# Other batches' mixing matrices on GpSimd, a later value chunk, and a fifth early product group in an attention and feed-forward kernel

## The chip, the cores and the metric

The kernel runs on one core of a Trainium2 chip. A core has five engines with an instruction queue each: TensorE (PE in the profile, with its weight loads as PEld), VectorE (DVE), ScalarE (ACT), GpSimd (POOL) and SyncE (SP). Each engine takes its instructions in order; semaphores order them between engines. Matrix products land in PSUM, which has eight banks of 2 KB for each of 128 partitions; GpSimd doesn't reach PSUM. The metric is the time of the whole program on the device in microseconds (us), lower is better. A profiled execution has a span, from the first to the last instruction that the profile shows, and a time of its own that is a little longer.

## The reference

Four batches, eight heads, 768 positions, head width 64. A sequence is cut into 8 blocks of 96. Per batch and head an 8x8 matrix is made from `sort_net` by five rounds of exponential and row and column normalisation; it mixes the key blocks and the value blocks. Attention then runs inside each block, and its output, heads side by side, goes through a gated feed-forward layer.

```
for _ in range(5):
    P = P - max(P, -1);  P = exp(P)
    P = P / (sum(P, -1) + 1e-09);  P = P / (sum(P, -2) + 1e-09)
k_sorted = einsum('bhij,bhjcd->bhicd', P, k_b)     # 8 blocks of 96 positions
v_sorted = einsum('bhij,bhjcd->bhicd', P, v_b)
attn = softmax(q_b @ k_sorted^T / 8);  x = attn @ v_sorted
x: 3072 tokens x 512
out = (silu(x @ w_gate) * (x @ w_val)) @ w_out      # 512 -> 1536 -> 512
```

## The kernel before, in words

Everything is in bfloat16 on the way into TensorE. The tokens are taken in eight groups of 384 (half a batch); a group `ffn(n)` has twelve gate products and twelve value products (four matmuls of 128x384 each, one for each 128 of the 512 channels `kc`), and the output products of the group before it. `gate_out` (L416) is a tanh on ScalarE (L420) and a product on VectorE (L422); `value_out` (L434) is one more product on VectorE (L435).

Attention is cut into units of two heads and four blocks. For a unit, `qk` makes the scores on TensorE (L334) and their exponentials on ScalarE (L345, L347); `av` (L353) averages the values on TensorE (L361), and VectorE divides by the sums with a reciprocal (L365) and a product (L367). For batch 0 the result is transposed on TensorE (L378) into x, drained to SBUF by a copy.

Before that, keys and values of batch 0 are mixed by TensorE: `w_ps` (L497) holds the spread 8x8 matrices of all batches, and `mix_rows` (L501) multiplies it by a 0/1 mask into the block matrices `rmix`, for batch 0 first and for batches 1 to 3 after the first scores (L524). `v_chunk` (L295) mixes 8 or 16 of the 64 value channels at a time, `k0_chunk` (L280) some of the 48 key positions of each half, `q0_chunk` (L271) only transposes q. Each chunk ends in a cast out of PSUM, on VectorE ("v") or ScalarE ("s") as its argument says. q of batch 0 is loaded in two halves; the second (`load_q0(1)`, L178) is used by `q0_chunk(1, ...)` (L634).

PSUM is shared out by tags: "a" and "b" are tiles of two banks, "gen" is three single banks in turn, "x" is one bank. A tile is given out again when the last reader of the one before it is done.

The order of the work in the opening (up to L573) is written out by hand for TensorE, GpSimd, VectorE and ScalarE. While x arrives slice by slice (`x_first`, L536), `early` (L546) runs matmuls of the first four products of group 0 (gates 0 and 1, values 0 and 1) for those slices that are there; the fourth has half of a two-bank tile "a". From L574 on the order is by hand for TensorE, GpSimd, ScalarE and SyncE, and a scheduler places VectorE's work. There `merge` (L604) lays side work into a product group by due times: a product counts 0.65, and a piece of side work is taken once the count has reached its due time. `units(0, range(4, 8), ...)` (L577, L637) is the second half of batch 0 in group 0: scores of two units, an average after 1.9 and 3.6, and the transpose 3.1 after each average.

The loads of weights, k, q and v are issued by GpSimd's queue in the order of the code; eight transfers can be under way, and the next waits for the oldest to land.

Of the kernel before, what the change touches and what calls it, by code (L numbers as in the profile page):

```python
# [10 lines left out]
BF16 = mybir.dt.bfloat16  # L11
# [6 lines left out]
def kernel(  # L18
# [11 lines left out]
    nc = tc.nc  # L30
# [80 lines left out]
    def load_k(b, lo, hi):  # L111
        load_groups(kq_tile(b), highr, k_nat[b], lo, hi)
# [5 lines left out]
    def load_q(b, lo, hi):  # L118
        load_groups(kq_tile(b), lowr, q_nat[b], lo, hi)
# [60 lines left out]
    load_gv(1024, DF)  # L180
    load_v(1, 0, 2)
    load_v(1, 2, 4)
    for lo, hi in ((0, 2), (2, 4)):
        load_k(1, lo, hi)
        load_q(1, lo, hi)
    for n in range(3):
        nc.gpsimd.dma_start(out=wo_sb[n], in_=wo_dram[:, n * 4:(n + 1) * 4, :])

    rmix = {b: const.tile([128, 2, H, NB], BF16, name=f"rmix{b}") for b in (0, 1, "p")}
    for t in rmix.values():  # L190
# [18 lines left out]
    rowreds = [const.tile([BH, NB, 1], FP32, name=f"rowred{it}") for it in range(N_ITER)]  # L209
    colred = const.tile([BH, 1, NB], FP32)  # L210
    p_bf = const.tile([BH, NB, 4, NB], BF16)
    def pair_tile(name, tag):
        return psum.tile([128, 1024], FP32, name=name, tag=tag)

    def bank_tile(name, tag="gen"):
        return psum.tile([128, 512], FP32, name=name, tag=tag, bufs=3 if tag == "gen" else 1)
# [54 lines left out]
    def q0_chunk(t, at, n, eng, tag):  # L271
        dst = kqt_tile(0)[:, GI * C:2 * GI * C].rearrange("p (g t r c) -> p t g r c", g=H2, t=2, c=QC)[:, t]
        tp = chunk_tile("tq0", n // 8, tag).rearrange("p (l g r) -> p l g r", l=n, g=H2)
        for lc in range(n):
            for two in range(2):
                nc.tensor.matmul(tp[two * D:(two + 1) * D, lc], lhsT=q0[t][:, at + lc, :],  # L276
                                 rhs=sel[:, two], start=True, stop=True)
        drain(eng, dst[:, :, :, at:at + n], tp.rearrange("p l g r -> p g r l"))

    def k0_chunk(at, n, eng, tag, parts=None):  # L280
        dst = kqt_tile(0)[:, 0:GI * C].rearrange("p (n a c) -> p a n c", a=2, c=HC)
        rm = rmix[0].rearrange("p a (g two) i -> p two a g i", two=2)
        tp = chunk_tile("tk0", n // 8, tag).rearrange("p (l a n) -> p l a n", l=n, a=2)
        for lc in range(n):
            for two in range(2):
                nc.tensor.matmul(tp[two * D:(two + 1) * D, lc].rearrange("p a (g i) -> p a g i", g=H2),
                                 lhsT=k0[:, at + lc, :], rhs=rm[:, two], start=True, stop=True)
        src = tp.rearrange("p l a n -> p a n l")
        if parts is None:
            drain(eng, dst[:, :, :, at:at + n], src)  # L290
            return
        drain(eng, dst[:, :, 0:parts, at:at + n], src[:, :, 0:parts])
        return lambda e: drain(e, dst[:, :, parts:, at:at + n], src[:, :, parts:])

    def v_chunk(b, at, n, eng, tag):  # L295
        rows = slice(0, 128) if b % 2 else lowr
        dst = vt_tile(b // 2)[:, b % 2]
        mix = rmix[b][rows, 0].rearrange("p a b -> p (a b)")
        tp = chunk_tile("tv", n // 8, tag).rearrange("p (l n) -> p l n", n=H * NB)
        for ld in range(n):  # L300
            col = (at + ld) * C
# [175 lines left out]
    def fill(tile, n):  # L477
        for _ in range(n):
            nc.tensor.matmul(tile, lhsT=warm_sb[:, 0:128], rhs=warm_sb, start=True, stop=True)  # L479
# [18 lines left out]
                             lhsT=p_bf[:, i].rearrange("p a b -> p (a b)"),  # L498
                             rhs=ident[0:BH, 0:BH], start=True, stop=True)

    def mix_rows(dst, rows, b):  # L501
        nc.vector.tensor_tensor(dst, mask[rows].unsqueeze(2).to_broadcast([R, H, NB]),
                                w_ps[rows, :, b].transpose([0, 2, 1]), op=ALU.mult)

    mix_rows(rmix[0][lowr, 0], lowr, 0)
    mix_rows(rmix[0][highr, 1], highr, 0)
    q0_chunk(0, 0, 16, "s", "b")
    v_chunk(0, 0, 8, "v", "gen")
    v_chunk(0, 8, 8, "s", "gen")
    v_chunk(0, 16, 16, "v", "a")  # L510
    v_chunk(0, 32, 8, "v", "gen")
    v_chunk(0, 40, 16, "s", "b")
    v_chunk(0, 56, 8, "s", "gen")
    q0_chunk(0, 16, 8, "v", "x")
    k0_chunk(0, 16, "s", "a")
    k0_chunk(16, 16, "v", "b")
    rest = [k0_chunk(at, 8, "s", "gen", 2 * NB) for at in (32, 40)]
    for drain_rest in rest:
        drain_rest("v")
    idle_ps = bank_tile("idle_ps", "x")  # L520
    fill(idle_ps, 3)
    qk(0, 0, "a")
    qk(0, 1, "b")
    for b in range(1, B):  # L524
        rows = halves[b % 2]
        mix_rows(rmix["p"][rows, b % 2] if b > 1 else rmix[1][rows, 0], rows, b)
    qk(0, 2, "gen")
    fill(idle_ps, 1)
    av(0, 0, "a")
    fill(idle_ps, 2)  # L530
    av(0, 1, "b")
    xts[(0, 0)] = xtp.tile([128, H2, TW], BF16, name="xt0_0", tag="xt")
    qk(0, 3, "mixed")
    av(0, 2, "a")

    def x_first(u, eng, tag):  # L536
        x_ps = xt_tile(tag, 1)[:, 0]
# [1 line left out]
        drain(eng, xts[(0, 0)][:, u, :], x_ps.rearrange("p a b -> p (a b)"))  # L539

    x_first(0, "s", "gen")
    x_first(1, "s", "gen")
    av(0, 3, "b")
    first = {}

    def early(n, kcs):  # L546
        sb, m, name = ((wg_sb, 0, "g_ps"), (wv_sb, 0, "v_ps"), (wg_sb, 1, "g_ps"), (wv_sb, 1, "v_ps"))[n]
        if n not in first:
            first[n] = (bank_tile(name) if n < 3 else pair_tile(name, "a"))[:, 0:TW]
        for kc in kcs:  # L550
            nc.tensor.matmul(first[n], lhsT=sb[:, kc, ts(m, 128)], rhs=xts[(0, 0)][:, kc, :],
                             start=(kc == 0), stop=(kc == NKC - 1))
# [2 lines left out]
    early(1, (0,))  # L555
    x_first(2, "s", "x")
    early(3, (0,))
    early(2, (0,))
    early(0, (1,))
    early(1, (1,))  # L560
    x_first(3, "v", "x")
    early(2, (1,))
    early(3, (1,))
    early(0, (2, 3))
    early(1, (2, 3))
    early(2, (2, 3))
    early(3, (2, 3))
    gate_out(0, 0, first[0])
    value_out(0, 0, first[1])
    gate_out(0, 1, first[2])  # L570
    value_out(0, 1, first[3])
    nc.vector.tensor_copy(rmix[1][lowr, 1].rearrange("p h i -> p (h i)"), ident[lowr, lowr])
    man.__exit__(None, None, None)  # L573
    man = tc.manual_schedule(engines={ET.PE, ET.Pool, ET.Activation, ET.SP})  # L574
# [42 lines left out]
    def ffn(n):  # L617
        todo = []
        for m in range(NFC):
            if n > 0 or m > 1:  # L620
                todo.append((0.65, lambda m=m: gate(n, m)))
                todo.append((0.65, lambda m=m: value(n, m)))
            ends = (7, 9, 11) if n == 1 else (3, 7, 11)
            if n > 0 and m in ends:
                for part in range(3):
                    todo.append((0.87, lambda t3=ends.index(m), part=part: outp(n - 1, t3, part)))
        return todo
# [62 lines left out]
```

## Time and profile before

| | us |
|---|---|
| median of three runs (lowest, highest) | 244.79 (244.59, 245.19) |
| the profiled execution | 244.99 |
| its span | 243.1 |
| TensorE busy | 235.4 |
| VectorE busy | 154.7 |
| ScalarE busy | 112.6 |
| GpSimd busy | 51.3 |

Times in the profile's rows are counted from the start of the span. A row of the timeline gives start, busy time, engine, line, operation, what it writes and reads, how many instructions it merges, and in brackets how long the engine sat idle before it and what ended that. A matmul's end is modelled and overlaps the next one's start, so the starts are what to read on TensorE.

### The profile page before, as it was taken

How to read it: one execution, taken by the hardware profiler on the slowest of the kernel's cores; microseconds unless marked ns; L12 is line 12 of the kernel's file. 1: busy time of each engine (PE TensorE's matmuls, PEld its weight loads, DVE VectorE, ACT ScalarE, POOL GpSimd, SP SyncE). 2: the span in 40 equal slices, each digit the busy share in tenths (PEclk: the TensorE clock that was granted, in tenths of full speed). 3: DMA queues.
4: the chain of work that ended last, by engine and by line, in shares of the span. 5: the costliest groups of instructions: out<-in, count | busy, mean ns of one | idle time of the engine just before them, and what ended most of it. 6: DMA issues, size and time to landing. Idle time of an engine off the chain costs nothing.

```text
span 243.1 us, 6156 instructions
## 1 busy us (share of the span) xinstructions
PE 235.4 (97%) x2613; PEld 138.5 (57%) x2613; DVE 154.7 (64%) x326; ACT 112.6 (46%) x191; POOL 51.3 (21%) x45
## 2 busy tenths in 40 slices
PE   7799999999999999999999999999999999999994
PEld 5375666676556566555555565565556555555543
DVE  6687789875665585866855855584576476445700
ACT  3976663486525544455453353254325434332312
POOL 5992229950006089000000000000000000000000
PEclk9999999999999999999999999999999999999999
DMA  5989999999926997543122212012111211110122
GB/s 93 214 131 209 206 213 212 205 210 193 156 78 107 219 177 109 109 95 81 49 72 61 47 45 80 0 59 63 32 43 49 73 36 43 43 43 3 43 86 86
DMA packets 39642, 24.77 MB, mean 102 GB/s; under 512 B 29376, under 2 KB 34368, under 8 KB 39616
## 3 DMA queue, kind: packets, MB, share of 16 engines
q0 software_dynamic: 19632, 14.16, 39.2%
q1 hardware_dynamic: 19840, 10.17, 15.8%
q8 instruction: 20, 0.33, 0.6%
q10 hardware_dynamic: 144, 0.07, 0.1%
q14 instruction: 6, 0.05, 0.1%
HBM read 28.32 MB, written 7.86 MB: 149 GB/s over the span
## 4 chain that ended last, share of the span: by engine, by line
PE 88%; DMA 6%; POOL 3%; DVE 1%; issue 0%; ACT 0%; POOLq 0%
PE v_ps L430 26%; PE g_ps L412 25%; PE o_ps L447 25%; DMA qk<-in_q_dram 4%; PE av_ps L361 3%; PE tkq L266 3%; PE qk L334 3%; POOL vch L148 3%; DMA v<-in_v_dram 2%; PE tv L312 1%; PE o_ps L463 1%; PE tv L302 1%; PE tq L276 0%; POOL wv_sb L134 0%; POOL wg_sb L134 0%
## 5 line engine op out<-in xcount | busy, mean ns | idle before, releaser
L422 DVE SCALAR_TENSOR_TENSOR gs_sb<-th_sb,g_ps 128x384 bf16<-128x384 bf16 x96 | 52.9, 552 | 50.8 <-ACT th_sb L420 47.8
L412 PE MATMUL g_ps<-xt,wg_sb 128*128 128x384 bf16 x376 | 76.6, 325 | 0.1
L430 PE MATMUL v_ps<-xt,wv_sb 128*128 128x384 bf16 x376 | 76.5, 326 | 0.0
L420 ACT ACTIVATE th_sb<-g_ps 128x384 bf16<-128x384 f32 x96 | 47.1, 491 | 57.3 <-PE g_ps L412 54.1
L447 PE MATMUL o_ps<-wo,h 128*128 128x512 bf16 x276 | 64.4, 379 | 0.0
L435 DVE SCALAR_TENSOR_TENSOR h<-v_ps,gs_sb 128x384 bf16<-128x384 f32 x96 | 53.4, 556 | 7.7 <-PE tkq L266 0.5
L412 PEld LDWEIGHTS <-wg_sb 128*128 128x128 bf16 x376 | 34.8, 97 | 23.4
L430 PEld LDWEIGHTS <-wv_sb 128*128 128x128 bf16 x376 | 35.0, 97 | 23.1 <-issue 0.2
L447 PEld LDWEIGHTS <-h 128*128 128x128 bf16 x276 | 26.0, 98 | 28.5
L452 ACT COPY o_sb<-o_ps 128x512 f32<-128x512 f32 x23 | 13.5, 586 | 49.3 <-PE o_ps L447 49.3
L148 POOL COPY vch<-v 64x1536 bf16<-64x1536 bf16 (+2 forms) x11 | 28.8, 2663 | 10.0 <-DMA v<-in_v_dram 10.0
L347 ACT ACTIVATE e_all<-qk 96x768 bf16<-96x768 f32 x30 | 23.2, 801 | 4.3 <-PE qk L334 4.3
L367 DVE TENSOR_TENSOR st<-av_ps,r_sb 96x512 bf16<-96x512 f32 x32 | 21.8, 680 | 0.3
L361 PEld LDWEIGHTS <-e_all 96*128 96x128 bf16 x256 | 11.9, 97 | 4.9 <-ACT e_all L347 0.6
L361 PE MATMUL av_ps<-vt,e_all 96*128 96x65 bf16 x256 | 13.0, 193 | 0.1
L246 ACT CAST vt<-tv 96x1024 bf16<-96x1024 f32 (+1 forms) x11 | 10.1, 931 | 4.7 <-PE tv L312 3.5
L365 DVE RECIPROCAL r_sb<-av_ps 96x8 f32<-96x8 f32 x32 | 6.4, 199 | 7.9 <-PE av_ps L361 7.9
L244 DVE CAST vt<-tv 96x1024 bf16<-96x1024 f32 (+1 forms) x7 | 7.4, 1065 | 2.2 <-PE tv L312 1.8
L479 PE MATMUL idle_ps<-warm_sb 128*128 128x512 bf16 x24 | 6.6, 382 | 0.0
L244 DVE COPY oq_v<-o_ps 128x128 f32<-128x128 f32 x1 | 0.3, 292 | 9.3 <-PE o_ps L463 9.3
L397 POOL DMA_DIRECT2D q_scr<-in_q_dram x2 | 5.6, 2813 | 0.3 <-issue 0.3
L146 ACT COPY vch<-v 64x768 bf16<-64x768 bf16 (+1 forms) x4 | 5.5, 1386 | 0.4 <-DMA v<-in_v_dram 0.4
(83 smaller groups left out, 130.5 us busy)
## 6 DMA issues: line engine op xcount, KB each, us to landing
out_dram<-o_sb SPq DMA_DIRECT2D x23, 256.0 KB, 2.0
v<-in_v_dram POOLq DMA_DIRECT2D x4, 384.0 KB, 12.7
wg_sb<-in_moe_w_gate_dram POOLq DMA_DIRECT2D x3, 512.0 KB, 11.2
wv_sb<-in_moe_w_val_dram POOLq DMA_DIRECT2D x3, 512.0 KB, 13.0
wo<-in_moe_w_out_dram POOLq DMA_DIRECT2D x3, 512.0 KB, 16.4
kqp<-in_k_dram POOLq DMA_DIRECT2D x2, 768.0 KB, 9.8
q_scr<-in_q_dram POOLq DMA_DIRECT2D x2, 768.0 KB, 17.4
v<-in_v_dram POOLq DMA_DIRECT2D x2, 768.0 KB, 9.8
```

Of the source, the lines that this page charges most:

```text
L148: eng.tensor_copy(dst, src.transpose([0, 2, 1]))
L246: nc.scalar.copy(dst, src)
L347: nc.scalar.activation(e_all[:, n:n + 2, 0:4 * C], wide[0:C, :, 0:4 * C], AF.Exp, scale=scale)
L361: nc.tensor.matmul(o[:, two, i4, 0:D + 1], lhsT=e[:, i4 * C:i4 * C + 128], rhs=vt[:, 2 * g + two, half * 4 + i4, 0:D + 1], start=True, sto ...
L367: nc.vector.tensor_tensor(st.rearrange("p i two d -> p two i d"), o[0:C, :, :, 0:D], r_sb.to_broadcast([C, 2, 4, D]), op=ALU.mult)
L412: nc.tensor.matmul(g_ps, lhsT=wg_sb[:, kc, ts(m, 128)], rhs=xt[:, kc, :], start=(kc == 0), stop=(kc == NKC - 1))
L420: nc.scalar.activation(th_sb, g_ps, AF.Tanh, scale=0.5)
L422: nc.vector.scalar_tensor_tensor(gs_sb, th_sb, 1.0, g_ps, op0=ALU.add, op1=ALU.mult)
L430: nc.tensor.matmul(v_ps, lhsT=wv_sb[:, kc, ts(m, 128)], rhs=xt[:, kc, :], start=(kc == 0), stop=(kc == NKC - 1))
L435: nc.vector.scalar_tensor_tensor(h_tiles[n][:, m, :], v_ps, 0.5, gs_tiles.pop(m), op0=ALU.mult, op1=ALU.mult)
L447: nc.tensor.matmul(o_ps, lhsT=h_w[:, m, ts(t3, 128)], rhs=wo_sb[part][:, m % 4, :], start=(m == 0), stop=(m == NFC - 1))
L452: nc.scalar.copy(o_sb, o_ps)
```

## The change

- `mix_rows` takes the engine and the source as arguments. Batch 0's matrices are still made by VectorE from `w_ps`. Right behind them VectorE copies the rest of `w_ps` to `w_sb` in SBUF, and GpSimd makes the matrices of batches 1 to 3 from that copy; they stand on its queue behind the loads of v of batch 1 and ahead of the loads of k and q of batch 1 and of the output weights.
- In the opening, the value chunk at channel 32 is drained by ScalarE, the small q chunk comes earlier, the two 8-wide key chunks come ahead of the two 16-wide ones, and the engines of these two are exchanged. The value chunk at channel 56 uses the bank "x" and stands behind the keys and the fills, and VectorE drains it.
- The first average stands ahead of the third unit's scores, and the first transposes stand ahead of the third and fourth averages.
- `early` runs five products: gate 2 joins, in the other half of the tile "a" that value 1 has. `ffn(0)` starts at value 2.
- `q0_chunk(1, ...)` moves into the opening behind the early products, and ScalarE drains both of its chunks.
- The due times of the second half of batch 0 go from 1.35 and 5.95 to 1.95 and 6.5.

```diff
@@ the loads
     load_v(1, 2, 4)
-    for lo, hi in ((0, 2), (2, 4)):
-        load_k(1, lo, hi)
-        load_q(1, lo, hi)
-    for n in range(3):
-        nc.gpsimd.dma_start(out=wo_sb[n], in_=wo_dram[:, n * 4:(n + 1) * 4, :])
...
+    w_sb = const.tile([128, NB, B, H], BF16)
...
-    def mix_rows(dst, rows, b):
-        nc.vector.tensor_tensor(dst, mask[rows].unsqueeze(2).to_broadcast([R, H, NB]),
-                                w_ps[rows, :, b].transpose([0, 2, 1]), op=ALU.mult)
-
-    mix_rows(rmix[0][lowr, 0], lowr, 0)
-    mix_rows(rmix[0][highr, 1], highr, 0)
+    def mix_rows(eng, dst, rows, w, b):
+        eng.tensor_tensor(dst, mask[rows].unsqueeze(2).to_broadcast([R, H, NB]),
+                          w[rows, :, b].transpose([0, 2, 1]), op=ALU.mult)
+
+    mix_rows(nc.vector, rmix[0][lowr, 0], lowr, w_ps, 0)
+    mix_rows(nc.vector, rmix[0][highr, 1], highr, w_ps, 0)
+    nc.vector.tensor_copy(w_sb[:, :, 1:], w_ps[:, :, 1:])
+    for b in range(1, B):
+        rows = halves[b % 2]
+        mix_rows(nc.gpsimd, rmix["p"][rows, b % 2] if b > 1 else rmix[1][rows, 0], rows, w_sb, b)
+    for lo, hi in ((0, 2), (2, 4)):
+        load_k(1, lo, hi)
+        load_q(1, lo, hi)
+    for n in range(3):
+        nc.gpsimd.dma_start(out=wo_sb[n], in_=wo_dram[:, n * 4:(n + 1) * 4, :])
+
     q0_chunk(0, 0, 16, "s", "b")
     v_chunk(0, 0, 8, "v", "gen")
     v_chunk(0, 8, 8, "s", "gen")
     v_chunk(0, 16, 16, "v", "a")
-    v_chunk(0, 32, 8, "v", "gen")
+    v_chunk(0, 32, 8, "s", "gen")
+    q0_chunk(0, 16, 8, "v", "x")
     v_chunk(0, 40, 16, "s", "b")
-    v_chunk(0, 56, 8, "s", "gen")
-    q0_chunk(0, 16, 8, "v", "x")
-    k0_chunk(0, 16, "s", "a")
-    k0_chunk(16, 16, "v", "b")
     rest = [k0_chunk(at, 8, "s", "gen", 2 * NB) for at in (32, 40)]
+    k0_chunk(0, 16, "v", "a")
+    k0_chunk(16, 16, "s", "b")
+    idle_ps = bank_tile("idle_ps", "x")
+    fill(idle_ps, 3)
+    v_chunk(0, 56, 8, "v", "x")
     for drain_rest in rest:
         drain_rest("v")
-    idle_ps = bank_tile("idle_ps", "x")
-    fill(idle_ps, 3)
     qk(0, 0, "a")
     qk(0, 1, "b")
-    for b in range(1, B):
-        rows = halves[b % 2]
-        mix_rows(rmix["p"][rows, b % 2] if b > 1 else rmix[1][rows, 0], rows, b)
-    qk(0, 2, "gen")
+    idle_ps = bank_tile("idle_ps", "x")
     fill(idle_ps, 1)
     av(0, 0, "a")
+    qk(0, 2, "gen")
     fill(idle_ps, 2)
     av(0, 1, "b")
...
     qk(0, 3, "mixed")
-    av(0, 2, "a")
...
     x_first(0, "s", "gen")
+    av(0, 2, "a")
     x_first(1, "s", "gen")
     av(0, 3, "b")
...
-        if n not in first:
-            first[n] = (bank_tile(name) if n < 3 else pair_tile(name, "a"))[:, 0:TW]
+        if n == 3 and n not in first:
+            wide = pair_tile("gv_ps", "a").rearrange("p (two n) -> p two n", two=2)
+            first[3], first[4] = wide[:, 0, 0:TW], wide[:, 1, 0:TW]
+        elif n not in first:
+            first[n] = bank_tile(name)[:, 0:TW]
...
     x_first(2, "s", "x")
     early(3, (0,))
+    early(4, (0,))
     early(2, (0,))
-    early(0, (1,))
-    early(1, (1,))
     x_first(3, "v", "x")
-    early(2, (1,))
-    early(3, (1,))
-    early(0, (2, 3))
-    early(1, (2, 3))
-    early(2, (2, 3))
-    early(3, (2, 3))
+    for n in range(5):
+        early(n, (1,))
+    for n in range(5):
+        early(n, (2, 3))
     gate_out(0, 0, first[0])
     value_out(0, 0, first[1])
     gate_out(0, 1, first[2])
     value_out(0, 1, first[3])
+    gate_out(0, 2, first[4])
+    q0_chunk(1, 0, 16, "s", "b")
+    q0_chunk(1, 16, 8, "s", "x")
...
         for m in range(NFC):
+            if n > 0 or m > 2:
+                todo.append((0.65, lambda m=m: gate(n, m)))
             if n > 0 or m > 1:
-                todo.append((0.65, lambda m=m: gate(n, m)))
                 todo.append((0.65, lambda m=m: value(n, m)))
...
-    q0_chunk(1, 0, 16, "s", "b")
-    q0_chunk(1, 16, 8, "v", "x")
-    merge(ffn(0), units(0, range(4, 8), (1.35, 5.95)))
+    merge(ffn(0), units(0, range(4, 8), (1.95, 6.5)))
```

More of the change, by code (lines that the diff above doesn't have):

```diff
@@ L546, in early @@
     def early(n, kcs):
-        sb, m, name = ((wg_sb, 0, "g_ps"), (wv_sb, 0, "v_ps"), (wg_sb, 1, "g_ps"), (wv_sb, 1, "v_ps"))[n]
-        if n not in first:
-            first[n] = (bank_tile(name) if n < 3 else pair_tile(name, "a"))[:, 0:TW]
+        sb, m, name = ((wg_sb, 0, "g_ps"), (wv_sb, 0, "v_ps"), (wg_sb, 1, "g_ps"), (wv_sb, 1, "v_ps"),
+                       (wg_sb, 2, "g_ps"))[n]
+        if n == 3 and n not in first:
[3 more added lines that the diff above has]
+            first[n] = bank_tile(name)[:, 0:TW]
         for kc in kcs:
```

## The prediction

> **What bounds the kernel.** I read the page's busy table first, then the table by stages, then the timelines of TensorE (PE), ScalarE (ACT) and VectorE (DVE) between 12 and 45 us, which are the stages that the change touches.
>
> ```profile
> span 243.1 us, 6156 instructions
> PE 235.4 (97%) x2613; PEld 138.5 (57%) x2613; DVE 154.7 (64%) x326; ACT 112.6 (46%) x191; POOL 51.3 (21%) x45
> ```
> ```profile
> 17.60:26.30 8.70, 8.00 (x148) 5.09 (x149) 6.00 (x17) 5.60 (x12) 2.57 (x6) 1.00 1.21 207
> 26.30:43.00 16.70, 16.63 (x167) 10.33 (x164) 15.40 (x36) 8.64 (x15) 9.36 (x8) 1.00 1.14 211
> 43.00:235.00 192.00, 191.99 (x1897) 110.37 (x1897) 120.56 (x228) 84.78 (x144) 24.64 (x13) 1.00 0.47 84
> ```
> In a stage's row the first figure is its length, then come busy us of PE, weight loads, DVE, ACT and POOL, and the granted clock. From 26.3 us on PE never rests (16.63 of 16.70, 191.99 of 192.00): what the opening loses or wins reaches the end unchanged. But from 26.3 to 43 us DVE is busy 15.40 of 16.70 as well: there is no room on it, so whatever waits for DVE there waits long.
>
> ```profile
> 24.01 0.22 PE L276 MATMUL tq<-sel,qk 128*64 128x64 bf16 x1 [0.28 <-DMA qk<-in_q_dram]
> 24.16 0.34 PE L551 MATMUL g_ps<-xt,wg_sb 128*128 128x384 bf16 x1
> ...
> 25.40 0.95 PE L276 MATMUL tq<-sel,qk 128*64 128x64 bf16 x47
> ...
> 28.34 0.51 PE L334 MATMUL qk<-kqt 64*128 64x96 bf16 x16
> ```
> On PE, one transposed-q matmul stands among the early products and waits for the second half of q (landed at 23.97: the chain of waits has it as 14.11 + 9.86). The last slice of x was there at 23.28 + 0.36 = 23.64, so about 0.45 us of products (24.16 against 23.70) is lost. At 28.34 come the scores of unit 4, the first to read that half of q.
>
> ```profile
> 24.53 0.49 ACT L420 ACTIVATE th_sb<-g_ps 128x384 bf16<-128x384 f32 x1 [1.68 <-PE g_ps L551]
> 25.18 0.49 ACT L420 ACTIVATE th_sb<-g_ps 128x384 bf16<-128x384 f32 x1 [0.16 <-PE g_ps L551]
> 26.13 1.01 ACT L246 CAST kqt<-tq 128x1024 bf16<-128x1024 f32 x1 [0.46 <-PE tq L276]
> 27.14 0.49 ACT L420 ACTIVATE th_sb<-g_ps 128x384 bf16<-128x384 f32 x1
> ```
> ```profile
> 25.06 0.56 DVE L422 SCALAR_TENSOR_TENSOR gs_sb<-th_sb,g_ps 128x384 bf16<-128x384 bf16 x1 [1.42 <-ACT th_sb L420]
> ...
> 26.85 0.56 DVE L435 SCALAR_TENSOR_TENSOR h<-v_ps,gs_sb 128x384 bf16<-128x384 f32 x1
> 27.33 0.17 DVE L572 COPY rmix<-ident 64x64 bf16<-64x64 bf16 x1
> 27.41 0.68 DVE L244 CAST kqt<-tq 128x512 bf16<-128x512 f32 x1
> ```
> ACT casts the larger q chunk at 26.13, as soon as it is made; DVE casts the smaller one at 27.41, behind h1 (the second value product, 26.85). The first tanh starts at 24.53 and h1 ends at 27.41: 2.88 us through two gates and two values.
>
> **The change, part by part.** The sum is made against the profiled execution: 244.99 us, a span of 243.1 and 1.9 around it; it stands 0.2 above the median of 244.79. Names: g and v with a number are the gate and value products (four matmuls, 0.65 us on PE by the starts 26.28, 26.94 and 27.59 of three such groups, so 0.163 for one), th, gs and h what ACT and DVE make of them.
>
> *Mixing matrices to GpSimd.* DVE loses three operations (0.22 + 0.45 us, 18.19 to 18.88) in front of a wait (its reciprocal at 19.35 sat idle 0.46 for PE), so this gives nothing on the path. DVE gains a copy of 128x192 out of PSUM. No row shows one; the mixing of 64x64 (0.22) and the cast of 128x256 (0.42) bound it. I take 0.35, nearer to the cast. It falls into the 0.42 us that DVE idles ahead of 12.85: cost 0, and with that cover gone 0.35 on a queue that has 0.4 to spare before the scores. GpSimd gains three 64x64 products; the nearest rows are its 0.25 us memset and its 0.68 us copy of 64x288, so 0.75 to 2.0 us. They run at 19.0, where the queue then idles 2.36 us until a wv_sb transfer has landed, before its next issue. Behind them stand four k and q loads and three of the output weights. The first of those takes 18.7 us to land (issue 21.37, so 40.1) and is used at 43.20: an overrun of 1 us would still cost nothing. SP's queue issues nothing in this stage.
>
> The Trainium skill's GPSIMD Engine Reference (Performance versus the Vector engine) speaks against this move: two-input elementwise work takes GpSimd about twice as long as DVE. By it the three would take about 1.3 us, an estimate, and still fit; no row here shows the operation.
>
> *Drains before the first scores.* The copy frees the bank of w_ps at about 12.8, so the chunk at channel 32 no longer waits (PE 13.32 to 13.59). But ACT gets that chunk, then 40 to 55 (cast 14.7 to 15.7), and the changed order lets the 16-wide key chunk into tile b only after that cast: keys 15.8 to 16.5 on PE, ACT's cast 16.5 to 17.5. Before, the last drain ended at 17.50 on DVE; the scores stay at 17.65. Value channels 56 to 63 and the key halves behind them occupy DVE until 18.85, ahead of the reciprocal at 19.35: covered.
>
> *Order of scores and averages.* Scores 2 now follow average 0, and the two fills (0.22 each) follow them, so average 1 goes from 19.59 to 19.87. DVE's chain of reciprocal 0.2 and product 0.69 slips 0.13; ACT's exponentials slip 0.28, and its copy of x slice 2 ends at 23.05 in place of 22.86. Slice 3 uses the same bank: 23.10 in place of 22.91. Loss 0.19.
>
> *Five products.* From 23.10: transposes 0.17, then fifteen matmuls, the last at 25.55, and q at 25.80 (0.25 of switching, as 25.15 to 25.40 before), its last matmul at 26.57. Before that was at 26.15. The DMA wait is gone, for q is asked for 1.8 us after it landed; what is late next is slice 3. PE is 0.42 later with 0.65 more done: **-0.23**.
>
> *A new wait.* v1 and g2 share one two-bank tile. In the built order the third tanh waits for a DVE semaphore: h1, which reads the other half of that tile. ACT's queue holds both q casts behind this tanh, since the change gives ACT the small one too. Chain: g0's last matmul 24.25, tanh 24.62, plus 2.88, h1 ends 27.50; tanh to 28.03, cast of 1.01 to 28.95, cast of 0.58 (ACT's time for 512 columns) to 29.43, scores at 29.47. PE is there at 26.57 + 0.13 + 3 x 0.65 + 0.1 = 28.75. Stall **+0.72**.
>
> The Trainium skill's PSUM page (PSUM bank collisions raise a hardware error) says that two engines on different banks run clean, and rows here agree: the tanh at 27.14 reads one bank while h1 (26.85 to 27.41) reads another. By that rule the hardware needs no such wait, and without it this stall would be 0 and the sum +1.0; the program's semaphores have it all the same.
>
> *Side work of the first product group.* It starts with one gate fewer, and the due times move by 0.6. In the built order one product group stands between average 5 and the scores of units 6 and 7, where two stood.
>
> ```profile
> 32.29 0.41 PE L361 MATMUL av_ps<-vt,e_all 96*128 96x65 bf16 x8
> ...
> 33.93 0.57 PE L334 MATMUL qk<-kqt 64*128 64x96 bf16 x16
> ```
> ```profile
> 32.83 0.20 DVE L365 RECIPROCAL r_sb<-av_ps 96x8 f32<-96x8 f32 x1
> 32.95 0.56 DVE L435 SCALAR_TENSOR_TENSOR h<-v_ps,gs_sb 128x384 bf16<-128x384 f32 x1
> 33.43 0.68 DVE L367 TENSOR_TENSOR st<-av_ps,r_sb 96x512 bf16<-96x512 f32 x1
> ```
> Scores 7 need tile a back, which DVE's last product of average 5 frees at 34.10, 1.81 us after that average began; PE came there after 1.84 us (33.93 and eight of the sixteen matmuls, 0.2), just in time. With one group fewer PE is there after 0.24 + 0.65 + 0.3 = 1.2, DVE still after 1.8: 0.62, less the 0.04 that the scores waited before, **+0.58**.
>
> At the end of the group the transposes of x slices 6 and 7 have one product between them where three stood, and the copy of slice 6 now stands behind gs11 on DVE.
>
> ```profile
> 41.27 0.35 DVE L244 COPY xt<-x_ps 128x384 bf16<-128x384 bf16 x1
> ...
> 42.07 0.55 DVE L422 SCALAR_TENSOR_TENSOR gs_sb<-th_sb,g_ps 128x384 bf16<-128x384 bf16 x1
> ```
> From g11's last matmul: 0.33 to its end, tanh 0.49, gs 0.55, copy 0.35 and three hand-overs, 1.76 us until slice 7 may use the bank; PE has 0.16 + 0.17 + 0.65 = 0.98 to do. Stall **+0.78**. The wait for slice 7's copy that PE has before (the first product of the next group takes 1.05 us at 42.22) shrinks by 0.11.
>
> The small q cast leaves DVE (0.68) for ACT (0.58): counted in the chain above. Sum: -0.23 + 0.72 + 0.58 + 0.78 - 0.11 = **+1.74**, so 246.7 in the profiled run and **246.5** against the median.
>
> **Rivals.** (A) Nothing measurable: the three stalls come to some 0.3 in all, because DVE, free of the 0.68 cast, runs ahead. For it: that cast is off DVE. Against it: the chains start at PE's own ends, and 15.40 of 16.70 leaves little. Time 244.6 to 245.5. (B) Faster: the idle 0.47 us of ACT at 14.48 leaves the path and the scores start that much earlier, with the stalls absent: -0.23 - 0.47 = -0.7, 244.1, and below with a little more. It decides only if ACT's key cast ends by 17.0; the reuse of tile b speaks against it. (C) Part of it: the wait for h1 and the bank of slice 6 hold, the one between is absorbed: +1.2 to +0.7, 245.5 to 246.0. (D) Worse: after the first stall DVE stays behind, and each later group adds some 0.3: 247.3 to 248. Against clock loss: PE has waited 0.9 us for DVE in this trace (idle_ps L489) at a granted clock of 1.00.
>
> **How the numbers follow.** Three runs of before span 0.6 us, so 0.3% (0.73 us) is about what can be told from no change. Forecast 0.60 (its own range 245.9 to 247.2: each stall by 0.2 and the slip of 0.19 by as much), C 0.17, A 0.11, B 0.05, D 0.07. C lies almost wholly past 245.5. Faster 0.06, same 0.13, slower 0.81. The range 245.3 to 247.3 leaves out B, most of A and most of D.
>
> **What would show it.** Right: PE free of the DMA wait at 24.0; ACT idle before the third tanh until h1 ends near 27.5; the first scores after q near 29.4; a gap of 0.6 inside the scores of units 6 and 7; slice 7's transposes 0.8 late behind the copy of slice 6; GpSimd's products inside 19 to 21.4. Wrong: if the third tanh runs at 26 the first stall is gone; if the scores start before 17.2 the opening won more than I gave it; if the table by stages shows PE at 97% through 26 to 43 us the stalls do not exist.

## The result, and the profile after

The changed kernel takes 247.35 us (median of six runs, 247.09 to 247.65), the kernel before, timed beside it, 244.99 us (six runs, 244.59 to 245.58): slower by the ratio 1.0092, 95% interval 1.0078 to 1.0106. That is 0.85 us above the forecast of 246.5 and 0.05 us past the upper end of its range. Part of this is the yardstick: the kernel before came out 0.20 us higher here than the 244.79 that the forecast was made against. As a difference it is 2.36 us, where 1.7 was forecast in a range of 0.5 to 2.5. The profiled execution took 247.59 us, 2.60 us more than the profiled one of before.

The head of the page of the changed kernel, and its table by stages (length; then busy us of PE, weight loads, DVE, ACT and POOL; then the granted clock):

```profile
span 245.2 us, 6158 instructions
...
PE 236.2 (96%) x2613; PEld 139.0 (57%) x2613; DVE 154.1 (63%) x323; ACT 113.0 (46%) x192; POOL 52.2 (21%) x48
```
```profile
17.60:27.16 9.56, 8.56 (x153) 5.50 (x152) 6.53 (x15) 5.44 (x11) 3.86 (x9) 1.00 1.21 206
27.16:45.40 18.24, 16.43 (x166) 10.09 (x162) 14.90 (x35) 9.09 (x16) 10.53 (x8) 1.00 1.15 208
45.40:237.40 192.00, 191.99 (x1898) 110.47 (x1898) 120.31 (x227) 84.88 (x144) 23.37 (x13) 1.00 0.45 82
```

The 192 us behind the first product group are as they were, at the same clock of 1.00. All of the loss that the trace shows lies ahead of 45.4 us. In the rest of the first group PE is busy 16.43 of 18.24 us, where it was busy 16.63 of 16.70. PE waits there in three places. Its timeline in the changed kernel (the number in brackets is the idle time ahead of the row, with what ended it):

```profile
22.50 0.34 PE L559 MATMUL v_ps<-xt,wv_sb 128*128 128x384 bf16 x1 [0.34 <-DMA wv_sb<-in_moe_w_val_dram]
...
26.27 0.95 PE L272 MATMUL tq<-sel,qk 128*64 128x64 bf16 x48
...
29.92 0.52 PE L330 MATMUL qk<-kqt 64*128 64x96 bf16 x16 [0.64 <-ACT kqt L242]
...
36.43 0.34 PE L330 MATMUL qk<-kqt 64*128 64x96 bf16 x8 [0.56 <-DVE st L363]
...
44.36 0.33 PE L374 MATMUL x_ps<-ident,st 96*128 96x96 bf16 x4 [0.61 <-DVE xt L240]
```

The bracket counts from a modelled end, so I measure a wait by the distance of two starts, less the usual distance for such a row. That gives 0.80 us ahead of the scores of unit 4 (29.92; 0.10 of it is usual when the kind of matmul changes, so 0.70), 0.75 between the scores of unit 6 and those of unit 7, called scores 7 below (36.43; 0.07 before, so 0.68), and 0.775 ahead of the transposes of slice 7 (44.36; none before). They end with ACT's cast, with DVE's product of an average and with DVE's copy: the three places of the forecast. The wait of 0.28 for the second half of q is gone, and all 48 transposed-q matmuls stand together. At 22.50 there is a wait that the kernel before did not show in its profile: the first value weights.

The first of the three, on ACT and on DVE:

```profile
25.73 0.49 ACT L416 ACTIVATE th_sb<-g_ps 128x384 bf16<-128x384 f32 x1 [0.16 <-PE g_ps L559]
27.98 0.49 ACT L416 ACTIVATE th_sb<-gv_ps 128x384 bf16<-128x384 f32 x1 [1.76 <-DVE h L431]
28.37 1.50 ACT L242 CAST kqt<-tq 128x1024 bf16<-128x1024 f32 x2
```
```profile
27.39 0.56 DVE L431 SCALAR_TENSOR_TENSOR h<-gv_ps,gs_sb 128x384 bf16<-128x384 f32 x1
28.50 0.56 DVE L418 SCALAR_TENSOR_TENSOR gs_sb<-th_sb,gv_ps 128x384 bf16<-128x384 bf16 x1 [0.56 <-ACT th_sb L416]
```

ACT idles 1.76 us until h1 (27.39 + 0.56) has read its half of the shared tile; both casts of q stand behind that tanh and end at 29.87, and the scores start at 29.92.

### The profile page after: what moved, and what is told of

It is laid out like the page before. It is cut to its first block, busy times and chain, and to the rows that moved or that the text cites. A ratio compares the mean times of both kernels' runs of the same rounds, so it can differ in the third digit from the quotient of the medians.

```text
span 245.2 us, 6158 instructions
## 1 busy us (share of the span) xinstructions
PE 236.2 (96%) x2613; PEld 139.0 (57%) x2613; DVE 154.1 (63%) x323; ACT 113.0 (46%) x192; POOL 52.2 (21%) x48
## 4 chain that ended last, share of the span: by engine, by line
PE 83%; DMA 7%; DVE 5%; POOL 2%; ACT 2%; issue 1%; DVEq 0%; ACTq 0%; POOLq 0%
PE o_ps L443 25%; PE v_ps L426 23%; PE g_ps L408 23%; DMA wv_sb<-in_moe_w_val_dram 4%; DMA v<-in_v_dram 3%; PE tkq L262 3%; PE qk L330 3%; PE av_ps L357 2%; DVE gs_sb L418 2%; DVE h L431 2%; POOL vch L148 1%; PE tv L308 1%; PE o_ps L459 1%; ACT th_sb L416 1%; PE tv L298 1%
## 5 line engine op out<-in xcount | busy, mean ns | idle before, releaser
L408 PE MATMUL g_ps<-xt,wg_sb 128*128 128x384 bf16 x372 | 75.8, 325 | 0.0
L431 DVE SCALAR_TENSOR_TENSOR h<-v_ps,gs_sb 128x384 bf16<-128x384 f32 x95 | 52.8, 556 | 7.8 <-PE v_ps L426 0.7
L475 PE MATMUL idle_ps<-warm_sb 128*128 128x512 bf16 x24 | 7.1, 405 | 0.4 <-DVE vt L240 0.4
L330 PE MATMUL qk<-kqt 64*128 64x96 bf16 x128 | 4.5, 204 | 1.2 <-ACT kqt L242 0.6
```

The lines of the kernel that those rows point to most:

```text
L330: nc.tensor.matmul(pss[two][:, i4 * C:(i4 + 1) * C], lhsT=k_sb[lo:lo + D, k_at + at:k_at + at + 128], rhs=q_sb[lo:lo + D, q_at + at:q_at + ...
L408: nc.tensor.matmul(g_ps, lhsT=wg_sb[:, kc, ts(m, 128)], rhs=xt[:, kc, :], start=(kc == 0), stop=(kc == NKC - 1))
L431: nc.vector.scalar_tensor_tensor(h_tiles[n][:, m, :], v_ps, 0.5, gs_tiles.pop(m), op0=ALU.mult, op1=ALU.mult)
```

## Where the time went, in all runs

PE's starts divide a run into three stretches: the opening (first scores to the last transposed-q matmul), the rest of the first product group (to the first k and q chunk of group 1, L262), and everything behind it. "Outside" is a run's time less its span, the mean over the runs of that kernel; it is the program's own and hardly scatters. Kernels with a fifth early product have 0.65 us more work in the opening and 0.65 less in the group.

| kernel | opening | group | behind | outside | time, median (before beside it) |
|---|---|---|---|---|---|
| before | 8.51 | 17.04 | 196.21 | 1.94 | 244.99 |
| before, again | 8.67 | 17.04 | 196.21 | 1.94 | 244.77 (244.98) |
| changed | 9.51 | 18.36 | 196.22 | 2.38 | 247.35 (244.99) |
| changed, again | 9.55 | 18.36 | 196.21 | 2.35 | 247.51 (244.98) |
| e1 gate ahead | 8.99 | 17.61 | 196.20 | 2.39 | 246.42 (244.78) |
| e2 due times | 9.62 | 17.20 | 196.20 | 2.36 | 246.01 (244.78) |
| e3 both | 8.99 | 16.43 | 196.20 | 2.37 | 245.18 (244.78) |
| e4 mixing alone | 8.54 | 17.05 | 196.21 | 2.18 | 244.97 (244.78) |
| e5 average 5 earlier | 8.99 | 18.12 | 196.56 | 2.38 | 247.72 (244.98) |
| e6 old opening | 8.48 | 16.43 | 196.19 | 2.35 | 244.55 (244.98) |
| e7 first due time | 8.99 | 17.91 | 196.19 | 2.34 | 246.87 (244.81) |
| e8 second due time | 8.99 | 17.88 | 196.56 | 2.36 | 247.24 (244.81) |
| f2 q in the opening | 8.02 | 17.04 | 196.18 | 2.38 | 244.93 (245.01) |

At equal work the group would take 17.04 - 0.65 = 16.39 us; the changed kernel's 18.36 is 1.97 too long.

## The experiments

The theory was the forecast's: three waits of some 0.7 us each, the first from the shared tile, the other two from the due times. Rivals: VectorE is the bound of this group and its backlog only moves from wait to wait; the mixing on GpSimd delays the loads; the new order of the opening costs more than it brings.

**e1, gate 2's tanh ahead of value 1.** Both halves of the tile "a" are as in the change, and only the order of their readers differs.

```
-    value_out(0, 1, first[3])
     gate_out(0, 2, first[4])
+    value_out(0, 1, first[3])
```

> The changed kernel with one line moved: the third gate's tanh and product come ahead of the second value product, so that the tanh on ScalarE no longer waits for VectorE. Theory (three stalls, this one 0.70 us): the scores of unit 4 start without the 0.80 us gap; the gap inside the scores of units 6 and 7 and the one ahead of slice 7's transposes stay at 0.6 to 0.8 each; 246.65 us. Rival (the q casts are late anyway, since ScalarE has both): the gap stays above 0.5 and the time within 0.3 of the changed kernel's 247.35. Rival (VectorE is the true limit): the 0.70 us comes back later in the group, 247.2 or more.

Measured: 246.42 us (246.25 to 246.76), ratio 1.0063 (1.0048 to 1.0078). ACT's timeline:

```profile
25.82 0.49 ACT L416 ACTIVATE th_sb<-gv_ps 128x384 bf16<-128x384 f32 x1 [0.16 <-PE gv_ps L559]
26.45 1.50 ACT L242 CAST kqt<-tq 128x1024 bf16<-128x1024 f32 x2
...
29.11 0.81 ACT L343 ACTIVATE e_all<-qk 96x768 bf16<-96x768 f32 x1 [0.51 <-PE qk L330]
```

The tanh follows PE instead of DVE, the casts end at 27.95, and the scores start at 28.66 with no wait. The group is 0.75 us shorter (18.36 to 17.61), and the two later waits stay (0.74 at 35.13, 0.775 at 43.05). So the first wait is the order of two readers of one tile, and its price was 0.75.

**e2, the old due times**, with everything else as changed.

```
-    merge(ffn(0), units(0, range(4, 8), (1.95, 6.5)))
+    merge(ffn(0), units(0, range(4, 8), (1.35, 5.95)))
```

> The changed kernel with the due times of batch 0's second half put back to 1.35 and 5.95. Theory: the averages and transposes stand as far from the next scores as in the kernel before, so the gap inside the scores of units 6 and 7 (0.75) and the one ahead of slice 7's transposes (0.78) go, while the first gap (0.80 ahead of unit 4's scores) stays; 245.9 us, and the wait for slice 7's copy is back at 0.1 to 0.25. Rival (VectorE's load, not the spacing): the gaps move to other places and the time stays above 246.7.

Measured: 246.01 us (245.84 to 246.74), ratio 1.0049 (1.0033 to 1.0066). The first wait stays at 0.80, the one at scores 7 shrinks from 0.75 to 0.19, the one at slice 7 is gone, and two of 0.15 are left at value 11 (the group's last value product, counted from 0) and at the next group's first gate. The group is 1.17 us shorter. The due times made the third wait and all but 0.12 of the second.

**e3, both edits together.**

> Both edits: the third gate's tanh ahead of the second value product, and the due times put back. Theory: the three gaps are gone and what is left is the opening, 0.2 us later on TensorE than before at equal work; 245.2 us, against 245.0 of the kernel before. If the late landing of the first value weights (22.45 against 21.08 us) was chance, 244.8. Rival (gaps that hide each other): 246 or more.

Measured: 245.18 us, ratio 1.0015 (1.0003 to 1.0026). The group is back to 16.43 us, 0.04 from the 16.39 at equal work; 0.75 + 1.17 = 1.92 removed apart, 1.93 removed together. The time is the 245.2 that I expected, in part by luck: the first value weights landed early here (20.44), for which I had expected 244.8, and the rest is time outside the span, which I had not counted. Its stage in the table by stages shows PE without a wait:

```profile
26.70:43.00 16.30, 16.30 (x166) 9.98 (x160) 14.26 (x35) 8.67 (x15) 8.99 (x8) 1.00 1.14 211
```

**e4, the mixing on GpSimd alone**: the kernel before with `mix_rows`, the copy `w_sb` and the loads as changed, nothing else.

> The kernel before with the mixing alone moved: batch 0's matrices by VectorE, the copy to SBUF, the other three by GpSimd ahead of the loads of k, q and output weights; everything else as before. Theory: free. GpSimd's three products take about 0.32 us each in its idle time; the bank of the spread matrices comes free earlier, which spares TensorE the 0.27 us wait ahead of the chunk at channel 32; 244.7 to 245.1 us. Rival (the move costs, by the copy on VectorE or by later weight loads): 245.5 or more, with the first value weights landing after 22 us here too.

Measured: 244.97 us, ratio 1.0011 (0.9994 to 1.0028): no change that can be told. But that is two effects. The span is 0.3 us shorter in the profile: the chunk at channel 32 no longer waits 0.27 for the bank of `w_ps`, and the first scores start at 17.38 instead of 17.65 (17.55 when before was profiled again). And the time outside the span is 0.24 longer (2.18; 2.14 to 2.24 in twelve runs). GpSimd's queue in the changed kernel:

```profile
20.71 0.32 POOL L498 TENSOR_TENSOR rmix<-mask,w_sb 64x64 bf16<-64x64 bf16 x1
21.11 0.70 POOL L498 TENSOR_TENSOR rmixp<-mask,w_sb 64x64 bf16<-64x64 bf16 x2
22.74 0.64 POOL L100 DMA_DIRECT2D kq<-in_k_dram  x1 [0.93 <-DMA wv_sb<-in_moe_w_val_dram]
```

The load behind the three products waits for an older transfer to land, not for the products; no later wait of PE comes from it.

**e5, average 5 one product earlier**, to split the second wait from the third.

```
-    merge(ffn(0), units(0, range(4, 8), (1.95, 6.5)))
+    merge(ffn(0), units(0, range(4, 8), (1.95, 6.5), (1.9, 3.2)))
```

> The changed kernel with average 5 (and 7) laid one product earlier, the due times otherwise as changed. My theory: the wait inside the scores of units 6 and 7 (0.75 us in the changed kernel) is the time that VectorE takes with average 5, so with one more product group behind that average it falls to 0.05 or less; the waits of 0.80 ahead of unit 4's scores and of 0.78 ahead of slice 7's transposes stay. Time 0.7 below the changed kernel, 246.7 where the changed kernel is at 247.35. Rival: VectorE is behind anyway in this group, and the wait only moves to the next reader of a tile: the time stays within 0.3 of the changed kernel's.

Measured: 247.72 us (247.12 to 247.97), ratio 1.0106 (1.0065 to 1.0148), no better than the changed kernel. My theory missed: the wait at scores 7 is 0.82, although two products stand where one stood. PE and DVE of e5:

```profile
33.25 0.41 PE L357 MATMUL av_ps<-vt,e_all 96*128 96x65 bf16 x8
...
35.88 0.34 PE L330 MATMUL qk<-kqt 64*128 64x96 bf16 x8 [0.64 <-DVE st L363]
```
```profile
34.03 0.54 DVE L418 SCALAR_TENSOR_TENSOR gs_sb<-th_sb,g_ps 128x384 bf16<-128x384 bf16 x1
34.49 0.20 DVE L361 RECIPROCAL r_sb<-av_ps 96x8 f32<-96x8 f32 x1
34.67 0.56 DVE L431 SCALAR_TENSOR_TENSOR h<-v_ps,gs_sb 128x384 bf16<-128x384 f32 x1
35.15 0.68 DVE L363 TENSOR_TENSOR st<-av_ps,r_sb 96x512 bf16<-96x512 f32 x1
```

DVE comes to average 5 1.24 us after it began on PE (33.25 to 34.49). In the changed kernel that was 0.59:

```profile
35.11 0.20 DVE L361 RECIPROCAL r_sb<-av_ps 96x8 f32<-96x8 f32 x1
35.23 0.55 DVE L431 SCALAR_TENSOR_TENSOR h<-v_ps,gs_sb 128x384 bf16<-128x384 f32 x1
35.70 0.68 DVE L363 TENSOR_TENSOR st<-av_ps,r_sb 96x512 bf16<-96x512 f32 x1
```

In both, DVE works without a break from 0.52 us ahead of average 4 on (31.19 in e5, 31.81 in the changed kernel), and takes the same operations in the same order up to the product that scores 7 wait for. From average 4 to scores 7 it needs 4.17 us in e5 and 4.10 in the changed kernel (32.33 to 36.43), PE without the wait 3.4: an earlier average 5 only queues longer. The rival that VectorE is behind in any case was right here. Two things went along that I had not foreseen. The wait of slice 7 fell to three small ones of 0.18, 0.08 and 0.24 (0.40 shorter in all), since averages 5 and 7 and slice 5 came earlier and left DVE freer at the end. And 0.36 of that was given back behind the group: in the third product group a gate waits 0.37 for one of DVE's value products, which no profile of before or of the changed kernel shows. PE's timeline in e5:

```profile
98.17 0.65 PE L408 MATMUL g_ps<-xt,wg_sb 128*128 128x384 bf16 x3 [0.21 <-DVE h L431]
```

**e7 and e8, one due time at a time**: `(1.35, 6.5)` and `(1.95, 5.95)` in the place of `(1.95, 6.5)`.

> The changed kernel with the first due time back at 1.35, the second left at 6.5: averages 4 and 5 come one product earlier, everything else on TensorE keeps its place. The run with average 5 alone one product earlier left the wait at scores 7 at 0.82 us, since VectorE came to that average 1.24 us after it began and not 0.59. My theory now: what sets that wait is how much TensorE work stands between average 4 (where VectorE's unbroken stretch starts) and scores 7: four products in the changed kernel, five here, so the wait falls by one product, from 0.70 net to 0.1 or less. The wait of 0.78 ahead of slice 7's transposes stays, since slices 6 and 7 keep one product between them. Time 0.6 to 0.7 below the changed kernel. Rival: the work between average 5 and scores 7 decides, as the prediction put it: 0.1 too here, but then nothing explains the run with average 5 alone. Second rival: VectorE's backlog is passed on, and slice 7's wait moves by more than 0.2 in either direction.

Measured: 246.87 us (246.62 to 247.41), ratio 1.0086 (1.0066 to 1.0105). Averages 4 and 5 both come one product earlier, five products stand between average 4 and scores 7 instead of four, and the second wait is gone. In e7 the transposes of slice 4 come ahead of scores 7 too (0.27 with the change of kind), but e2 has the same five products without them, and 0.12 is left there. With e5 that settles it: what counts is how much of PE's work stands behind average 4, since there DVE's unbroken stretch begins, and not behind average 5. The wait of slice 7 did not stay where I had put it, though; it rose by 0.20, to 0.97, so the gain in the group is 0.45 and not 0.7. PE and DVE of e7 at the end of the group:

```profile
41.71 0.34 PE L374 MATMUL x_ps<-ident,st 96*128 96x96 bf16 x4
...
43.50 0.33 PE L374 MATMUL x_ps<-ident,st 96*128 96x96 bf16 x4 [0.81 <-DVE xt L240]
```
```profile
42.65 0.54 DVE L418 SCALAR_TENSOR_TENSOR gs_sb<-th_sb,g_ps 128x384 bf16<-128x384 bf16 x1
43.11 0.34 DVE L240 COPY xt<-x_ps 128x384 bf16<-128x384 bf16 x1
```

Here too the copy of slice 6, transposed at 41.71, waits behind the last gate's product on DVE until 43.11.

> The changed kernel with the second due time back at 5.95, the first left at 1.95: average 7 and the transposes of slice 6 come one product earlier, the scores stay. My theory: slice 7's transposes wait for the copy of slice 6, which stood behind the last gate's product on VectorE, and with two products between the slices that wait of 0.78 is gone (0.1 or less), while the wait at scores 7 stays at 0.70 to 0.75 and the one ahead of unit 4's scores at 0.80. Time 0.6 to 0.8 below the changed kernel. Rival: the backlog that scores 7 shows is carried to the end of the group, and the wait moves to the first product of the next group or to slice 7's own copy: the time is within 0.3 of the changed kernel's.

Measured: 247.24 us (247.07 to 247.50), ratio 1.0101 (1.0082 to 1.0120). By the trace my theory held: with two products between slices 6 and 7 the transposes of slice 7 don't wait, the waits at unit 4 and at scores 7 are 0.80 and 0.75 as before. Of the 0.775, 0.27 came back as a wait at value 11, so the group gains 0.48. By the time the rival's figure held, though by a wait in another place: the gate in the third group waits 0.37 here as well (behind: 196.56), and 0.1 to 0.3 is left. Alone, the two due times bring 0.45 + 0.48 = 0.93 in the group, together (e2) 1.17: each also clears what the other leaves. PE at the end of e8's group, and VectorE in the third group:

```profile
42.84 0.81 PE L426 MATMUL v_ps<-xt,wv_sb 128*128 128x384 bf16 x4
43.49 0.34 PE L374 MATMUL x_ps<-ident,st 96*128 96x96 bf16 x4
```
```profile
97.58 0.56 DVE L431 SCALAR_TENSOR_TENSOR h<-v_ps,gs_sb 128x384 bf16<-128x384 f32 x1 [0.46 <-PE g_ps L408]
```

This is the value product that the gate waits for: VectorE itself sat idle for 0.46 ahead of it, by the row for matmuls of a gate. In the changed kernel the same product (98.06) starts with no such wait, though VectorE has the same operations in the same order behind the first group; why the wait is there is open.

**e6, the old opening with five products**: both edits of e3, the kernel before's order of drains, scores, averages and transposes, and two of the slice-1 products back ahead of slice 3.

```
-    x_first(3, "v", "x")
-    for n in range(5):
+    early(0, (1,))
+    early(1, (1,))
+    x_first(3, "v", "x")
+    for n in range(2, 5):
         early(n, (1,))
```

> Both edits of the earlier runs (gate 2 ahead of value 1, due times as before), and the opening's order as the kernel before has it (drains, scores and averages, transposes), with the first two slice-1 products back ahead of slice 3; the five products, GpSimd's mixing and the q chunks in the opening stay. My theory: the new order of the opening cost 0.28 by the distance from the first scores to slice 3 and 0.2 by a later first score, so the first k and q chunk of group 1 starts at 42.4 to 42.6 instead of 43.0, and the time is 244.4 to 244.8, 0.3 to 0.7 below the kernel before. Rival: the products that fill the opening wait for the weights or for q instead, and nothing of it is left: 245.2, as with both edits alone.

Measured: 244.55 us (twelve runs, 244.35 to 245.41) against 244.98, ratio 0.9981 (0.9962 to 0.9999). The opening with 0.65 us more work takes 8.48, no longer than before's with four products; against the changed order (8.99) that is 0.51 us. Its group:

```profile
26.10:42.40 16.30, 16.30 (x166) 9.98 (x162) 14.26 (x35) 8.65 (x15) 9.18 (x8) 1.00 1.15 211
```

This version is below both kernels, by 0.2% against before; that is less than the 0.3% that I took as what can be told, and the interval just leaves out 1. In the profiles its span is 0.9 us shorter than before's (242.2 against 243.1), and 0.41 of that goes to the time outside.

**The two kernels again**, unaltered, in one session.

> The changed kernel unaltered. My theory: the landing of the first value weights at 22.45 (0.50 us wait on TensorE) and the 2.4 us outside the span vary by chance between executions; the three waits of 0.70 to 0.80 are the change's own and come again within 0.05. The time 247.2 to 247.5. Rival: the change itself makes the weights late, and they land after 22.2 here too.

> The kernel before unaltered, in the same session. My theory: the landing of the first value weights scatters between 20.4 and 22.6 here too, and the time outside the span between 1.9 and 2.4; the ratio to itself is 1.000 within 0.002. Rival: it lands at 21.1 and leaves 1.93 outside the span as in its first profile, which would lay both to the change.

Measured: the changed kernel 247.51 us, ratio 1.0095 (1.0063 to 1.0126), the kernel before against itself 0.9993 (0.9974 to 1.0011). The three waits come again at 0.80, 0.75 and 0.77. Two things that I had laid to chance come out differently.

The landing of the first value weights does vary by itself: it is at 22.45 and 22.59 in the two profiles of the changed kernel and at 22.64 in e2, at 20.4 to 20.7 in those of e1, e3, e5, e7 and e8, whose loads are the same, and in the kernel before at 21.08 and 22.21. But its price differs. The kernel before, again, and the changed kernel, again:

```profile
22.25 0.34 PE L551 MATMUL v_ps<-xt,wv_sb 128*128 128x384 bf16 x1 [0.42 <-DMA wv_sb<-in_moe_w_val_dram]
```
```profile
22.64 0.34 PE L559 MATMUL v_ps<-xt,wv_sb 128*128 128x384 bf16 x1 [0.39 <-DMA wv_sb<-in_moe_w_val_dram]
```

Both profiles of the changed kernel have the late landing, as the rival had it. That it lands early there too was not profiled; it is argued from the variants, and from the spans of 244.7 to 245.3 in its other executions. Both kernels lose some 0.55 us in these two rows. Before's opening is only 0.16 longer for it (8.67 against 8.51), since it then waits less for q; the changed kernel, without a wait for q to use up, is 0.5 longer (9.5 against the 8.99 of its variants).

The time outside the span does not vary: 1.88 to 2.08 us in all runs of before, 2.30 to 2.44 in all of the changed kernel and its variants. The rival was right, and 0.42 us of the loss belongs to the change, in a place where the trace shows nothing. The last two runs looked for it.

**f1**: e4 with the three products on VectorE, from the same copy. **f2**: e4 with the second half of q transposed in the opening and both of its chunks cast by ScalarE.

```
-        mix_rows(nc.gpsimd, rmix["p"][rows, b % 2] if b > 1 else rmix[1][rows, 0], rows, w_sb, b)
+        mix_rows(nc.vector, rmix["p"][rows, b % 2] if b > 1 else rmix[1][rows, 0], rows, w_sb, b)
```
```
     value_out(0, 1, first[3])
+    q0_chunk(1, 0, 16, "s", "b")
+    q0_chunk(1, 16, 8, "s", "x")
...
-    q0_chunk(1, 0, 16, "s", "b")
-    q0_chunk(1, 16, 8, "v", "x")
```

> The kernel before with the copy to SBUF and the moved loads, but all mixing matrices made by VectorE from that copy: no GpSimd product. In all runs so far the time outside the span is the program's own: 1.94 us in the kernel before (1.89 to 2.08), 2.18 with the mixing on GpSimd alone, 2.36 in the changed kernel and its variants. My theory: the 0.24 comes with GpSimd's three products (a kind of instruction that GpSimd does not have otherwise), so it is 1.94 here. Rival: it comes with the other tile in SBUF or the moved loads, so it is 2.18 here as well. The time: three products of 0.22 on VectorE ahead of the casts of value and key chunks move the first scores by 0.2 to 0.5 us, so 245.0 to 245.4.

> The mixing on GpSimd alone (0.24 outside the span, time 244.97) and with it the second half of q in the opening, both of its chunks cast by ScalarE; four early products, the old opening and the old due times. My theory: with gate 2 not in a shared tile nothing holds the third tanh, so the scores of unit 4 wait less than 0.1 us; the q chunk on TensorE stands behind the fourth product in both orders: 244.8 to 245.2. The time outside the span stays 2.18 if the fifth product or the opening brings the other 0.18, and is 2.36 if the place and the engine of the q chunks bring it. Rival for the time: ScalarE's two casts delay the tanh of gate 2 and so the work behind it, 245.3 or more.

Measured: f1 245.12 us, ratio 1.0014 (0.9990 to 1.0039), outside 1.96 (1.90 to 2.03). f2 244.93 us, ratio 0.9998 (0.9983 to 1.0013), outside 2.38 (2.33 to 2.45). So 0.22 to 0.24 us outside the span come with GpSimd's three products, not with the copy or the moved loads, and 0.20 more with the place or the engine of q's second half; fifth product, drains and due times bring none. What the chip does in that time stays open. Inside the span f2 is the better opening, 0.49 shorter than before's: q no longer stands among the early products, and no transfer is waited for.

The profiled execution of f1 took 247.53 us, far from its median, so its trace isn't in the table. It shows something else that went with a late landing. The first value weights landed at 23.20, PE waited for them, and from 23.53 on the granted clock (the third figure from the end of the stage's row) was 0.50 for 3.4 us:

```profile
23.25 0.34 PE L554 MATMUL v_ps<-xt,wv_sb 128*128 128x384 bf16 x1 [0.90 <-DMA wv_sb<-in_moe_w_val_dram]
```
```profile
23.53:26.94 3.41, 3.41 (x19) 1.71 (x17) 0.36 (x1) 0.48 (x1) 1.14 (x2) 0.50 1.24 207
```

Its opening took 10.63 us, its group (17.04) and the stretch behind (196.22) are those of the kernel before. Whether the wait brought the lower clock was not tested.

## Why the prediction was right, and what it missed

The direction, the places and the mechanism held; the size was put 0.65 us too low by the medians (1.7 against 2.36) and 0.86 by the profiled executions. By its steps:

- **The three waits and the slip at slice 7's copy.** Forecast 0.72 + 0.58 + 0.78 - 0.11 = 1.97; the group became 18.36 - 16.39 = 1.97 us longer. Singly 0.70, 0.68, 0.775 and -0.11 (0.12 in place of 0.23 ahead of the third matmul of the next group's first gate). The rest, -0.08, is spread over small switches; that the sums agree to the hundredth is luck.
- **The new wait** is shown by e1: the order of readers on one tile costs 0.75. The part of the working that drew on the Trainium skill (PSUM — Partial Sum Buffer, on PSUM bank collisions) stays untried: in no run here did two engines read the two banks of this tile at the same time, so that the hardware would allow it here is the page's word alone.
- **Scores 7** had nearly the right size for a reason that was too narrow. "One product group fewer between average 5 and the scores" fits the changed kernel, but e5 gives that group back and the wait stays. The step that failed is taking DVE's 1.8 us for average 5 as fixed: it is 1.91 in the changed kernel and 2.63 in e5 (33.25 to 35.88), because DVE is busy from average 4 on. e7 shows that the first due time decides it.
- **Slice 7** was right in cause and size (e8), and its wait is not independent of the others: 0.775 became 0.97 in e7 and some 0.5, spread over three places, in e5.
- **Opening, -0.23.** In the changed kernel's profile it was +0.22 (27.03 - 26.15 - 0.65). With the weights there in time it was -0.12 to -0.40 in five variants with the same opening, -0.23 in the middle. By its length the opening was 0.17 shorter at equal work in each of them (8.99 - 8.51 - 0.65); the scatter is in when the first scores start (17.42 to 17.69). The term was nearly right for that case; the step left out was the loads. I costed the vanished wait for q as a gain and did not ask what a late landing would cost without it: 0.5 here, 0.16 before. The argument against a loss of clock, that PE had waited 0.9 us at a granted clock of 1.00, held in the changed kernel, but in f1 a wait of 0.90 was followed by a clock of 0.50. The loss of 0.19 by the order of scores and averages measured 0.28 (first scores to slice 3: 5.26 before, 5.54 in e1 and e3).
- **Outside the span.** The sum was made with the same 1.9 us around the span. That term, costed at nothing, is +0.42. With the late landing it makes up the 0.86 us between the forecast's +1.74 and the +2.60 of the two profiled executions.
- **Mixing on GpSimd: 0.** Right in the time (e4, 1.0011), by two errors that cancel: the first scores came 0.27 earlier, and 0.24 was added outside. The copy took 0.36 where I had put 0.35. GpSimd's products ended at 21.81, past the 21.4 that I had given them, and PE did not wait for them. The Trainium skill's GPSIMD Engine Reference (Performance versus the Vector engine) has GpSimd at about twice VectorE's time for two-input elementwise work; here a 64x64 product took GpSimd 0.32 us. VectorE took 0.22 for it out of PSUM, and 0.26 to 0.34 from the same copy in SBUF as GpSimd's (f1), so like for like the ratio was below 1.3.
- **Rivals.** Nothing measurable, faster, and part of it fell with the three waits of 0.7 each. That VectorE stays behind was given 0.07; it is true inside the first group (e5, e7), but in the changed kernel nothing of it reached the later groups, where the stretch behind takes 196.2 us in both kernels.

## What to carry to other kernels

Where one engine has no idle time left, a wait on it can't be worked out from the nearest instruction: go back to where its unbroken stretch begins and count the other engine's work from there. Two results in one tile are two readers in one order, so put the reader first that others are queued behind. And compare the time less the span of both kernels before adding up a trace: an edit can cost there what it brings inside.

## What the runs showed of the hardware

- The time outside the span is constant for a program to about 0.1 us and differs between programs: 1.94 in before, 2.18 with three small products on GpSimd, 2.38 with q's second half in the opening as well. I had not expected an edit to move it.
- The same loads in the same order landed 2.2 us apart: the first value weights at 20.44 us in e3 and at 22.64 in e2. The kernel before, with another wait behind it, lost 0.16 by a late landing (22.21), the changed kernel 0.5.
- In f1's profile the granted clock was 0.50 for 3.4 us, right behind a wait of 0.90 us on TensorE for those weights; a wait of 0.85 us in the profile of the kernel before (at 8.50) and those of 0.56 to 0.64 in the changed kernel left it at 1.00. No run here shows what decides it.
- Two edits of the due times in the first product group (e5, e8) went with a wait of 0.37 us some 54 us later, in the third. VectorE's work there is placed by the scheduler, in the same order as in the changed kernel; how the one leads to the other is open.
